# Attention in delta-rule form: triangles used as 32x32 tiles on TensorE's diagonal instead of block-diagonal 128x128 copies

## The chip, the cores and the metric

One NeuronCore of a Trainium2 chip. The metric is the device time of one execution in microseconds (us): 1447.51 us as the median of 3 runs (1442.47 to 1449.78) for the kernel before. TensorE (PE) multiplies and accumulates into PSUM, VectorE (DVE), ScalarE (ACT) and GpSimd (POOL) work elementwise, SyncE (SP) issues most DMAs. Every engine takes its own instructions in order.

## What is computed

The reference is a delta-rule attention, then two mixtures of experts (an argmax-gated one of 8 experts, a dense one of 4):

```python
for t in range(S):                      # S = 768, 32 heads (4 x 8), D = 48
    kt, vt, bt = k_n[:, :, t], v[:, :, t], beta[:, :, t, None]
    y[:, :, t] = einsum('bhd,bhde->bhe', q[:, :, t], state)
    v_old = einsum('bhde,bhd->bhe', state, kt)
    state = state + bt[..., None] * einsum('bhd,bhe->bhde', kt, vt - v_old)
x = moe(x)    # one expert of 8 per token: relu(x @ w1[e]) @ w2[e], times two gates
x = moe2(x)   # four experts, weighted by domain_probs
```

## The kernel before

The recurrence is done by blocks of 32 tokens. `run` walks 6 chunks of 128 tokens (c), each of 4 steps of 32 tokens (st = 4c+s), in two head groups (g). For a block of 32 tokens the state's updates are a triangular system, so the kernel inverts a 32x32 triangle for each head and block: `gram` makes the triangles' entries on PE, `inverse` (L339) runs the elimination on DVE, 31 columns one after another (L356, L357), two buffers deep (`NX`), between a first transpose (L344) and a last one (L380). Beside the inverse X each head has a second triangle P (from q and k). Both are split into two fp16 halves, high by ACT and low by POOL (by DVE for the first chunk), and written to the dense tile `TPd` ([128, 2, 4, 16, 32]: f is a pair of steps, the index of 4 is X high, X low, P high, P low). A partition holds 4 heads' rows, 32 each.

`stage_t` (L395) copies `TPd` to one of two block-diagonal tiles `TP`, for each pair of steps by 4 DMAs from SP, one for each quarter of the partitions, so that a 128x128 weight holds four heads' triangles and zeros elsewhere. `zero` clears the two tiles once.

A step's chain (`chain`, L411): `inject` puts v into PSUM (L409), L424 subtracts keys times state (weights `KT`), ACT and DVE split the result into r16, L432 multiplies by the inverse (weights `TP`), ACT and DVE split that into u16, L444 updates the state (weights `kb`), ACT and DVE make S16 for the next step. `outputs` (L448) makes y: L461 with `QT` and S16, L467 with P (`TP`) and u16. Each product has three matmuls (`HL`): high by high, low by high, high by low. L432 is given in two parts: 8 matmuls on r16's high half, 4 on its low half.

The order on all engines is not the source's: each piece of work is registered by `op` with a duration in ns, a priority and what it reads and writes, and `Plan.order` simulates the engines and emits instructions in that order. A step's chain is urgent, the inversion has a priority of 25 steps ahead, `OFF` shifts single pieces. A copy by `stage_t` counts `TPX` = 900 ns in that plan, a matmul `PEN` = 25 or `PY` = 43. Where PE would stand idle, the plan puts in matmuls on zeros (L195).

The attention takes the first 470 us of the span, then follow the two mixtures with plans of their own. Their buffers lie where the attention's were.

Of the kernel before, what the change touches and what calls it, by code (L numbers as in the profile page):

```python
# [7 lines left out]
F16 = mybir.dt.float16  # L8
# [3 lines left out]
ALU = mybir.AluOpType  # L12
# [3 lines left out]
B, H, S, D = 4, 8, 768, 48  # L16
# [25 lines left out]
TPX = 900  # L42
# [8 lines left out]
NX = 2  # L51
# [106 lines left out]
class Attention:  # L158
# [7 lines left out]
    def __init__(self,ctx,tc,plan,q,k,v,beta,kq,wa,wb,done,nsc=NSC):  # L166
# [4 lines left out]
        T=lambda n,s,d=F32: c.tile(s,d,name=n)  # L171
# [166 lines left out]
    def inverse(self,c):  # L338

        TPv=self.TPd.rearrange("p f w (s u) i -> p f w s u i",s=2)  # L340
        nc=self.nc; G,Pm,TPd,X,GZ=self.GT,self.Pm,self.TPd,self.X[c%NX],self.GX[c%NX]; xi=c%NX; t=f"inv {c}"; self.prio=4*c-LEAD[3]
        Pf=Pm.rearrange("p (u f s) i -> p f s u i",f=2,s=2)
# [63 lines left out]
    def inject(self,st,g):
# [44 lines left out]
    def outputs(self,st,g):  # L451
        nc=self.nc; s=st%4
        qt=self.QT[st%self.RQ]; tpt=self.TP[st//2%self.RT]; tp=lambda w,u: tpt[:,w,8*(s%2)+u]
        us=range(4*g,4*g+4); o=4*g; t=f"out {st} {g}"; self.prio=st+0.3
        S16=self.S16[g][st%2]; ko=('S16',g,st%2); u16=self.u16[g][st%2]; ku=('u16',g,st%2); cy=('cp',g,0)
        yp=self.cp[g][0][:,0,0:8*D].rearrange("p (u a d) -> p u a d",a=2,d=D)
        for half in range(2):
            uh=us[2*half:2*half+2]
            def qs(uh=uh):
                for u in uh:  # L460
                    for a,b in self.HL: nc.tensor.matmul(out=yp[:,u-o],lhsT=qt[:,a,u],rhs=S16[:,b,u-o],start=(u,a,b)==(o,0,0),stop=False,skip_group_check=True)  # L461
            if st>0: self.op('P',6*PY,qs,self.QTk(st)+[ko+(x,p) for x in range(2) for p in range(2)],[cy],t)
        for half in range(2):
            uh=us[2*half:2*half+2]
            def pu(uh=uh):
                for u in uh:
                    for a,b in self.HL: nc.tensor.matmul(out=yp[:,u-o],lhsT=tp(2+a,u),rhs=u16[:,b,u-o:u-o+1].to_broadcast([128,2,D]),start=(st,u,a,b)==(0,o,0,0),stop=b==1,skip_group_check=True)  # L467
            self.op('P',6*PY,pu,self.TPk(st)+[ku+(0,),ku+(1,)],[cy],t)
        ys=self.ys[st%2]
        for pp in range(2):  # L470
            R=slice(64*pp,64*pp+64)
            self.act(211,ys[R,o:o+4],yp[R,:,pp],[cy],[('ys',st%2,g,pp)],t,scale=-1.0/512)

    def run(self):
        n=self.nsc; L=4*n
        self.load_b(0); self.loads(0); self.setup(); self.keys(0); self.gram(0); self.inverse(0)
        for i in range(3): self.load_v(i)
        self.stage_k(0); self.stage_t(0); self.stage_q(0); self.stage_q(1)
        if n>1: self.load_b(1); self.loads(1); self.keys(1); self.gram(1)
        for c in range(n):  # L480
            for s in range(4):
                st=4*c+s
                if s==0: self.stage_t(st+2)
# [11 lines left out]
                if s==2 and c+1<n: self.stage_t(st+2); self.stage_q(st+2)  # L495
def bc(ap,shape,axis):
# [531 lines left out]
```

## Time and profile before

| | |
|---|---|
| median of 3 runs | 1447.51 us |
| profiled execution: time, span | 1452.08 us, 1450.5 us |
| PE busy, matmuls | 1289.6 us (89%), 14904 |
| DVE, ACT, POOL busy | 930.2, 690.9, 714.4 us |
| mean granted TensorE clock | 0.927 of full |

The span runs from the first to the last instruction. The chain of waits goes back from the last instruction to whatever released it, and so on. Busy shares are means over stages with different limits; what counts in a stage is who ends last there.

### The profile page before, as it was taken

What the parts mean: (1) busy time and instruction counts of PE and PEld (TensorE: products, weight loads), DVE (VectorE), ACT (ScalarE), POOL (GpSimd) and SP (SyncE); (2) the same over time, 40 slices, a digit from 0 to 9 for tenths busy, and PEclk for the clock granted to TensorE, in tenths of its full rate; (3) what the DMA queues carried; (4) which work ended last, traced back from release to release, by engine and by line L of the source; (5) the groups of instructions that cost most, each with busy time, mean ns of one, the idle gap of its engine ahead of it and who ended that gap; (6) DMA issues with size and microseconds to landing.
All of it is one profiled execution on the core that took longest, in us unless ns stands there. A gap on an engine that the chain in (4) does not pass through costs nothing.

```text
span 1450.5 us, 35997 instructions
## 1 busy us (share of the span) xinstructions
PE 1289.6 (89%) x14904; PEld 1066.8 (74%) x14904; DVE 930.2 (64%) x1877; ACT 690.9 (48%) x1348; POOL 714.4 (49%) x927
## 2 busy tenths in 40 slices
PE   7677686777778798899989999999999999999997
PEld 4355475665566654455679999899998999999997
DVE  7979888859745556653285556855578555564654
ACT  2846464645464444542254444544445444444433
POOL 3445554533223478310185445744468444456664
PEclk8688878868889999999999999999999999999999
DMA  8968988794797786763220102101121011011200
GB/s 124 184 94 159 109 132 113 124 128 84 123 116 128 190 226 173 211 177 101 74 63 23 45 23 87 46 23 35 33 77 34 23 34 34 23 36 54 66 34 34
DMA packets 358888, 130.48 MB, mean 90 GB/s; under 512 B 314688, under 2 KB 348992, under 8 KB 358720
## 3 DMA queue, kind: packets, MB, share of 16 engines
q1 hardware_dynamic: 351856, 112.69, 40.4%
q0 software_dynamic: 6864, 15.45, 3.3%
q8 instruction: 118, 1.93, 0.6%
q14 instruction: 50, 0.41, 0.1%
HBM read 76.38 MB, written 14.96 MB: 63 GB/s over the span
## 4 chain that ended last, share of the span: by engine, by line
PE 50%; DVE 13%; DMA 11%; issue 11%; SPq 5%; POOL 5%; ACT 4%; another core or an unknown queue 0%; POOLq 0%; ACTq 0%; DVEq 0%
PE b L928 23%; PE b L947 20%; SPq L215 4%; DMA s<-in_moe_w_dram 4%; DMA TP<-TPd 4%; DVE tmp L356 2%; DMA kq<-wa 2%; PE b L800 1%; POOL q L775 1%; DVE KT L306 1%; POOL S L936 1%; DVE X L357 1%; DVE wa L357 1%; PE Sp L444 1%; DVE v L753 1%
## 5 line engine op out<-in xcount | busy, mean ns | idle before, releaser
L928 PE MATMUL b<-wb,v 128*128 128x256 f16 x3456 | 392.8, 273 | 0.3 <-ACT a L930 0.2
L928 PEld LDWEIGHTS <-v 128*128 128x128 f16 x3456 | 336.7, 98 | 37.9 <-issue 0.9
L947 PE MATMUL b<-v,h 128*128 128x192 f16 x4032 | 353.5, 247 | 11.6 <-DVE cc L955 6.4
L947 PEld LDWEIGHTS <-h 128*128 128x128 f16 x4032 | 338.7, 98 | 16.6 <-issue 8.6
L936 POOL TENSOR_TENSOR S<-a 128x256 f32<-128x256 f32 x192 | 149.7, 800 | 272.7 <-ACT a L930 272.5
L940 DVE TENSOR_TENSOR h<-a,h 128x768 f16<-128x768 f32 x96 | 135.0, 1407 | 145.8 <-ACT h L939 138.3
L940 DVE TENSOR_TENSOR h<-S,h 128x1024 f16<-128x1024 f32 x96 | 120.9, 1259 | 125.6 <-ACT h L939 125.6
L939 ACT ACTIVATE h<-S 128x1024 f16<-128x1024 f32 x96 | 101.4, 1056 | 199.5 <-POOL S L936 179.8
L930 ACT ACTIVATE a<-b 128x512 f32<-128x512 f32 x192 | 113.4, 594 | 143.8 <-PE b L928 134.8
L936 POOL TENSOR_TENSOR S<-S,a 128x256 f32<-128x256 f32 x96 | 133.8, 1394 | 0.0
L195 PE MATMUL wp<-wz 128*128 128x512 f16 x304 | 85.4, 424 | 10.1 <-DVE LG L556 7.4
L939 ACT ACTIVATE h<-a 128x768 f16<-128x768 f32 x96 | 80.8, 842 | 2.8
L936 POOL TENSOR_TENSOR S<-a,S 128x256 f32<-128x256 f32 x96 | 73.7, 768 | 7.2
L195 PEld LDWEIGHTS <-wz 128*128 128x128 f16 x398 | 40.6, 107 | 47.0 <-issue 18.0
L203 ACT ACTIVATE QT<-kq 64x512 f16<-64x512 f16 x96 | 60.0, 626 | 11.4 <-PE cp L461 6.5
L815 POOL DMA_DIRECT2D x<-y x27 | 19.7, 733 | 90.5 <-DVE y L813 80.8
L432 PE MATMUL cp<-r,TP 128*128 128x48 f16 x576 | 31.4, 198 | 36.8 <-DMA TP<-TPd 20.6
L803 DVE SCALAR_TENSOR_TENSOR h<-b,h 128x432 f16<-128x432 f32 (+2 forms) x72 | 39.6, 552 | 36.2 <-ACT h L802 35.3
L444 PE MATMUL Sp<-u,kb 64*128 64x48 f16 x1152 | 35.4, 193 | 29.4 <-DVE S L449 15.2
L955 DVE TENSOR_TENSOR cc<-b,sm 128x192 f32<-128x192 f32 x192 | 58.5, 345 | 3.1 <-ACT sm L952 3.1
L753 DVE SCALAR_TENSOR_TENSOR v<-s,v 128x512 f16<-128x512 f32 (+2 forms) x56 | 45.5, 840 | 23.0 <-ACT v L752 21.1
L550 POOL TENSOR_TENSOR ys<-ys,sc 128x384 f32<-128x384 f32 x24 | 20.9, 871 | 79.7 <-ACT xr L203 36.0
(249 smaller groups left out, 2145.6 us busy)
## 6 DMA issues: line engine op xcount, KB each, us to landing
wb<-x SPq DMA_DIRECT2D x72, 256.0 KB
s<-in_moe_w_dram SPq DMA_DIRECT2D x40, 384.0 KB
s<-in_moe_w_dram SPq DMA_DIRECT2D x18, 512.0 KB
TP<-TPd SPq DMA_DIRECT2D x48, 128.0 KB
s<-in_moe_w_dram SPq DMA_DIRECT2D x24, 256.0 KB
v<-in_v_dram SPq DMA_DIRECT2D x96, 48.0 KB
xd<-xr SPq DMA_DIRECT2D x24, 192.0 KB
x<-y POOLq DMA_DIRECT2D x21, 216.0 KB
```

The costliest lines, as they stand in the source:

```text
L195: nc.tensor.matmul(out=out,lhsT=wz[:,0:128],rhs=wz[:,0:out.shape[1]],start=start,stop=True,skip_group_check=True)
L203: self.op('A',dur,lambda: self.nc.scalar.activation(out=out,in_=in_,func=func,scale=scale),reads,writes,tag,**k)
L215: self.op(q,occ,(lambda: e.dma_start_transpose(out=out,in_=in_)) if turn else (lambda: e.dma_start(out=out,in_=in_)),reads,list(writes)+[( ...
L444: for a,b in ps: nc.tensor.matmul(out=Sp[:,pp,u],lhsT=kb[R,a,u],rhs=u16[R,b,u-o],start=(st,u,a,b)==(0,0,0,0),stop=last and b==1,skip_group ...
L753: self.op('V',69+1.042*n,lambda: self.nc.vector.scalar_tensor_tensor(out=lo,in0=s,scalar=64.0,in1=hi,op0=ALU.mult,op1=ALU.subtract),reads+ ...
L928: for c,y in PASS: nc.tensor.matmul(out=F[k][:,f],lhsT=w[:,c,d,c_:c_+128],rhs=self.xk[B%2][d][:,y,256*i:256*i+256],start=(f,z)==(0,0),stop ...
L930: self.op('A',620,lambda k=k,g=g: A.activation(out=a[ja][:,g].rearrange("p x t -> p (x t)"),in_=F[k].rearrange("p a t -> p (a t)"),func=AF ...
L936: self.op('G',750,lambda o=o,x=x,y=y,w=w: G.tensor_tensor(out=X[o],in0=X[x],in1=X[y],op=w),ka,[ks])
L939: self.op('A',200+.833*m,lambda h=h,q=q,g=g: A.activation(out=h[:,0,:,q],in_=g,func=AF.Copy),kg,[kh+(0,)])
L940: self.op('V',200+1.042*m,lambda h=h,q=q,g=g: V.tensor_tensor(out=h[:,1,:,q],in0=g,in1=h[:,0,:,q],op=ALU.subtract),kg+[kh+(0,)],[kh+(1,)])
L947: for z,(c,d) in enumerate(PASS): nc.tensor.matmul(out=Q[k][:,o,0:192],lhsT=h[:,c,g,x],rhs=w[:,d,m,y],start=(m,o,z)==(0,0,0),stop=(m,z)==( ...
L955: self.op('V',340,lambda o=o,k=k,y=y,x=x: V.tensor_tensor(out=o,in0=Q[k][:,y,0:192],in1=s[:,x],op=ALU.add),[('Q',k),('sm',z,x)],[ko])
```

## The change

`TP`, `stage_t` and the copies are gone. PE takes the triangles from `TPd` directly, with 4 matmuls for each one of before, each with a weight of 32 rows and 32 columns at partitions 32q and an output at the same partitions. `TPd` is now two tiles, one for even and one for odd chunks. The plan counts 12 ns for one such matmul. `OFF` is the same.

```diff
-        self.TP=[T(f"TP{i}",[128,4,16,128],F16) for i in range(self.RT)]
-        self.TPd=T("TPd",[128,2,4,16,32],F16)
+        self.TPd=[T(f"TPd{i}",[128,2,4,16,32],F16) for i in range(2)]
...
+    def diagonal(self,out,w,st,rhs,us,ps,start,n=1):
+        tp=self.TPd[st//4%2][:,st%4//2]; x=8*(st%2); o=us[0]-us[0]%4
+        for u in us:
+            for a,b in ps:
+                for q in range(4):
+                    R=slice(32*q,32*q+32); r=rhs[R,b,u-o]; r=r if n==1 else rhs[R,b,u-o:u-o+1].to_broadcast([32,n,D])
+                    self.nc.tensor.matmul(out=out[R,u-o],lhsT=tp[R,w+a,x+u],rhs=r,start=start and (u,a,b)==(o,0,0),stop=b==1,skip_group_check=True)
+    def TDk(self,st,w): return [('TPd',st//4%2,st%4//2,x) for x in (w,w+1)]
...
-    def stage_t(self,st):
-        c,s=divmod(st,4); self.prio=st-2; sl=st//2%self.RT; tp=self.TP[sl]; f=s//2
-        self.zero(tp,('TP',sl),[('TP',sl,q) for q in range(4)],'G' if sl else 'V')
-        for qq in range(4):
-            R=slice(32*qq,32*qq+32)
-            self.dma(tp[R,:,:,32*qq:32*qq+32].rearrange("p w u i -> p (w u) i"),self.TPd[R,f].rearrange("p w u i -> p (w u) i"),[('TPd',f,w) for w in range(4)],[('TP',sl,qq)],f"tp {st}",xfer=TPX)
...
-                    for a,b in ps: nc.tensor.matmul(out=up[:,u-o],lhsT=tp(a,u),rhs=r16[:,b,u-o],start=(u,a,b)==(o,0,0),stop=b==1,skip_group_check=True)
-            self.op('P',4*len(ps)*PEN,mm,self.TPk(st)+[kr+(x,)],[cu],t,**U)
+            self.op('P',16*len(ps)*12,lambda ps=ps,x=x: self.diagonal(up,0,st,r16,list(us),ps,x==0),self.TDk(st,0)+[kr+(x,)],[cu],t,**U)
...
-                    for a,b in self.HL: nc.tensor.matmul(out=yp[:,u-o],lhsT=tp(2+a,u),rhs=u16[:,b,u-o:u-o+1].to_broadcast([128,2,D]),start=(st,u,a,b)==(0,o,0,0),stop=b==1,skip_group_check=True)
-            self.op('P',6*PY,pu,self.TPk(st)+[ku+(0,),ku+(1,)],[cy],t)
+            self.op('P',24*12,lambda uh=uh: self.diagonal(yp,2,st,u16,list(uh),self.HL,st==0,2),self.TDk(st,2)+[ku+(0,),ku+(1,)],[cy],t)
```

In the program PE has 4608 pairs of weight load and matmul at the new line L397 for the 1152 pairs of L432 and L467, and 321 matmuls on zeros for 398. SP has 48 DMAs fewer.

In a step of the second chunk a weight load and a matmul of L432 (`TP_98`, 128x48) stood 8 times in a row on PE, then, behind matmuls of the other group, 4 times; now a pair of L397 (`TPd_112`, 32x48) stands there 32 and then 16 times.

ACT at the start of the second chunk (`TPd<-Pm` is P's high half of the next chunk, `u` the high half of u16, `S` that of the state), before and then now:

```order
L203 ACTIVATE wa<-qf 128x8x48 x4
L203 ACTIVATE TPd<-Pm 128x512
L203 ACTIVATE u_122<-cp_141 128x192
L203 ACTIVATE u_124<-cp_143 128x192
L203 ACTIVATE S_127<-Sp 128x4x48 x2
```

```order
L202 ACTIVATE TPd_112<-GX_108 128x512 x2
L202 ACTIVATE TPd_111<-Pm 128x512
L345 ACTIVATE X_109<-b_88 128x32
L202 ACTIVATE GT<-gp_138 128x8x32
L202 ACTIVATE Pm<-gp_138 128x8x32
L202 ACTIVATE QT_96<-kq 64x16x32
L202 ACTIVATE u_121<-cp_140 128x192
```

The write of the next chunk's P goes to the other tile now and has moved ahead, right behind the writes of this chunk's X.

SP at the start of the second chunk, before and then now:

```order
L215 DMA_TRANSPOSE kq<-wa 128x32x128
L215 DMA TP_98<-TPd 32x64x32 x4
L215 DMA v_116<-in_v_dram 32x8x48 x4
L215 DMA xd<-xr_152 128x768
L215 DMA xd<-xr_150 128x768
L215 DMA xd<-xr_151 128x768
L215 DMA TP_99<-TPd 32x64x32 x4
L215 DMA_TRANSPOSE kb_114<-KT_93 128x16x128
```

```order
L214 DMA_TRANSPOSE kq<-wa 128x32x128
L214 DMA_TRANSPOSE kb_113<-KT_93 128x16x128
L214 DMA v_116<-in_v_dram 32x8x48 x4
L214 DMA_TRANSPOSE kb_114<-KT_94 128x16x128
L214 DMA v_117<-in_v_dram 32x8x48 x4
L214 DMA_TRANSPOSE kq<-wa 128x32x128
```

The transposes of keys (`kb`, `kq`) stand closer together and no longer behind copies.

## Rows read from the trace of the kernel before

**Rows 1.** The page's chain that ended last, shares of the span by line.

```profile
PE b L928 23%; PE b L947 20%; SPq L215 4%; DMA s<-in_moe_w_dram 4%; DMA TP<-TPd 4%; DVE tmp L356 2%; DMA kq<-wa 2%; PE b L800 1%; POOL q L775 1%; DVE KT L306 1%; POOL S L936 1%; DVE X L357 1%; DVE wa L357 1%; PE Sp L444 1%; DVE v L753 1%
```

**Rows 2.** Windows, attention and ten us of it: us, busy us by engine, clock, DMA.

```profile
core 0: us, PE busy (x) PEld busy (x) DVE busy (x) ACT busy (x) POOL busy (x), PEclk, DMA share, GB/s
83.00:470.00 387.00, 289.93 (x5352) 232.16 (x5351) 292.56 (x771) 212.71 (x547) 163.76 (x208) 0.81 0.83 122
...
252.00:262.00 10.00, 8.74 (x246) 7.66 (x244) 9.74 (x24) 9.33 (x26) 5.15 (x6) 1.00 0.96 147
```

**Rows 3.** Chain of waits in order of time, 80 to 470: start us, us, what.

```profile
92.79 6.05 DMA TP<-TPd
...
153.43 5.27 DMA TP<-TPd
...
164.31 13.09 DMA TP<-TPd
...
298.05 14.26 DMA kq<-wa
...
365.61 10.11 DMA TP<-TPd
...
420.10 11.83 DMA kb<-KT
```

**Rows 4.** Who waited for whom, 50 to 470: us, times, longest us.

```profile
ACT TPd L203 <- DMA TP<-TPd: 42.7, 8, 13.4
...
PE cp L432 <- DMA TP<-TPd: 20.6, 5, 8.8
...
PEld L424 <- issue: 13.3, 47, 0.6
```

**Rows 5.** Timeline of DVE: start us, us, line, operation, [idle before <-releaser].

```profile
93.09 0.84 DVE L436 SCALAR_TENSOR_TENSOR u<-cp,u 128x192 f16<-128x192 f32 x2 [1.80 <-ACT u L203]
...
178.38 0.36 DVE L436 SCALAR_TENSOR_TENSOR u<-cp,u 128x192 f16<-128x192 f32 x1 [4.34 <-ACT u L203]
...
243.63 0.36 DVE L206 TENSOR_TENSOR r<-cp,r 128x192 f16<-128x192 f32 x1 [3.85 <-ACT r L203]
...
292.26 0.83 DVE L436 SCALAR_TENSOR_TENSOR u<-cp,u 128x192 f16<-128x192 f32 x2 [2.88 <-ACT u L203]
...
376.83 0.84 DVE L436 SCALAR_TENSOR_TENSOR u<-cp,u 128x192 f16<-128x192 f32 x2 [5.85 <-ACT u L203]
```

**Rows 6.** Timelines of DVE, POOL and PE at the last chunk's start.

```profile
402.29 1.98 DVE L380 STREAM_TRANSPOSE GX<-X 128x1024 f32<-128x1024 f32 x1
...
405.94 2.27 POOL L206 TENSOR_TENSOR TPd<-GX,TPd 128x512 f16<-128x512 f32 x2 [8.46 <-ACT TPd L203]
...
418.26 1.12 PE L432 MATMUL cp<-r,TP 128*128 128x48 f16 x24 [2.38 <-DMA TP<-TPd]
```

**Rows 7.** DMA, 92 to 465: packets, and one group of issues.

```profile
DMA packets 220981, 46.18 MB, mean 124 GB/s; under 512 B 215095, under 2 KB 220060, under 8 KB 220924
...
TP<-TPd SPq DMA_DIRECT2D x42, 128.0 KB
```

**Rows 8.** Timeline of PE, 250 to 275.

```profile
254.26 0.36 PE L432 MATMUL cp<-r,TP 128*128 128x48 f16 x8
...
254.96 0.44 PE L424 MATMUL cp<-S,KT 128*64 128x48 f16 x16
255.33 0.27 PE L432 MATMUL cp<-r,TP 128*128 128x48 f16 x4
255.53 0.31 PE L424 MATMUL cp<-S,KT 128*64 128x48 f16 x8
...
258.49 0.67 PE L467 MATMUL cp<-u,TP 128*128 128x96 f16 x12
...
262.91 0.42 PE L467 MATMUL cp<-u,TP 128*128 128x96 f16 x6
```

**Rows 9.** Windows, the matmuls on zeros (L195) alone: us, PE, PEld, clock.

```profile
83.00:470.00 387.00, 54.15 (x213) 21.49 (x212) 0.81 0.83 122
```

More of the change, by code (lines that the diff above doesn't have):

```diff
@@ L338, in inverse @@
     def inverse(self,c):
-        TPv=self.TPd.rearrange("p f w (s u) i -> p f w s u i",s=2)
-        nc=self.nc; G,Pm,TPd,X,GZ=self.GT,self.Pm,self.TPd,self.X[c%NX],self.GX[c%NX]; xi=c%NX; t=f"inv {c}"; self.prio=4*c-LEAD[3]
+        TPv=self.TPd[c%2].rearrange("p f w (s u) i -> p f w s u i",s=2); it=c%2
+        nc=self.nc; G,Pm,TPd,X,GZ=self.GT,self.Pm,None,self.X[c%NX],self.GX[c%NX]; xi=c%NX; t=f"inv {c}"; self.prio=4*c-LEAD[3]
         Pf=Pm.rearrange("p (u f s) i -> p f s u i",f=2,s=2)
@@ L383, in inverse @@
             pk=[('Pm',2*f),('Pm',2*f+1)]
-            self.act(520,TPv[:,f,2],Pf[:,f],pk,[('TPd',f,2)],t)
-            self.tt(EL,DL,TPv[:,f,3],Pf[:,f],TPv[:,f,2],ALU.subtract,pk+[('TPd',f,2)],[('TPd',f,3)],t)
+            self.act(520,TPv[:,f,2],Pf[:,f],pk,[('TPd',it,f,2)],t)
+            self.tt(EL,DL,TPv[:,f,3],Pf[:,f],TPv[:,f,2],ALU.subtract,pk+[('TPd',it,f,2)],[('TPd',it,f,3)],t)
         Xf=XT.rearrange("p (u f s) i -> p f s u i",f=2,s=2)
         for f in range(2):
-            self.act(520,TPv[:,f,0],Xf[:,f],[kg],[('TPd',f,0)],t)
-            self.tt(EL,DL,TPv[:,f,1],Xf[:,f],TPv[:,f,0],ALU.subtract,[kg,('TPd',f,0)],[('TPd',f,1)],t)
+            self.act(520,TPv[:,f,0],Xf[:,f],[kg],[('TPd',it,f,0)],t)
+            self.tt(EL,DL,TPv[:,f,1],Xf[:,f],TPv[:,f,0],ALU.subtract,[kg,('TPd',it,f,0)],[('TPd',it,f,1)],t)
+    def diagonal(self,out,w,st,rhs,us,ps,start,n=1):
[6 more added lines that the diff above has]
+    def TDk(self,st,w): return [('TPd',st//4%2,st%4//2,x) for x in (w,w+1)]
     def stage_k(self,st):
@@ L403, in stage_q @@
         self.spread(st,1,self.QT[st%self.RQ],'QT',SPQ,f"Qsp {st}")
-    def TPk(self,st): return [('TP',st//2%self.RT,q) for q in range(4)]
     def inject(self,st,g):
@@ L412, in chain @@
         nc=self.nc; s=st%4; last=st==4*self.nsc-1
-        kt=self.KT[st%self.RK]; tpt=self.TP[st//2%self.RT]; tp=lambda w,u: tpt[:,w,8*(s%2)+u]; kb=self.kb[st%2]
+        kt=self.KT[st%self.RK]; kb=self.kb[st%2]
         us=range(4*g,4*g+4); o=4*g; t=f"ch {st} {g}"; self.prio=st; U=dict(urgent=True)
@@ L429, in chain @@
         for x,ps in enumerate((self.HL[:2],self.HL[2:])):
-            def mm(ps=ps):
-                for u in us:
-                    for a,b in ps: nc.tensor.matmul(out=up[:,u-o],lhsT=tp(a,u),rhs=r16[:,b,u-o],start=(u,a,b)==(o,0,0),stop=b==1,skip_group_check=True)
-            self.op('P',4*len(ps)*PEN,mm,self.TPk(st)+[kr+(x,)],[cu],t,**U)
+            self.op('P',16*len(ps)*12,lambda ps=ps,x=x: self.diagonal(up,0,st,r16,list(us),ps,x==0),self.TDk(st,0)+[kr+(x,)],[cu],t,**U)
         u16=self.u16[g][st%2]; ku=('u16',g,st%2)
@@ L452, in outputs @@
         nc=self.nc; s=st%4
-        qt=self.QT[st%self.RQ]; tpt=self.TP[st//2%self.RT]; tp=lambda w,u: tpt[:,w,8*(s%2)+u]
+        qt=self.QT[st%self.RQ]
         us=range(4*g,4*g+4); o=4*g; t=f"out {st} {g}"; self.prio=st+0.3
@@ L464, in outputs @@
             uh=us[2*half:2*half+2]
-            def pu(uh=uh):
-                for u in uh:
-                    for a,b in self.HL: nc.tensor.matmul(out=yp[:,u-o],lhsT=tp(2+a,u),rhs=u16[:,b,u-o:u-o+1].to_broadcast([128,2,D]),start=(st,u,a,b)==(0,o,0,0),stop=b==1,skip_group_check=True)
-            self.op('P',6*PY,pu,self.TPk(st)+[ku+(0,),ku+(1,)],[cy],t)
+            self.op('P',24*12,lambda uh=uh: self.diagonal(yp,2,st,u16,list(uh),self.HL,st==0,2),self.TDk(st,2)+[ku+(0,),ku+(1,)],[cy],t)
         ys=self.ys[st%2]
@@ L477, in run @@
         for i in range(3): self.load_v(i)
-        self.stage_k(0); self.stage_t(0); self.stage_q(0); self.stage_q(1)
+        self.stage_k(0); self.stage_q(0); self.stage_q(1)
         if n>1: self.load_b(1); self.loads(1); self.keys(1); self.gram(1)
@@ L482, in run @@
                 st=4*c+s
-                if s==0: self.stage_t(st+2)
                 if s==0 and c+1<n: self.inverse(c+1)
@@ L494, in run @@
                 self.done(st,self.ys[st%2].rearrange('p u d -> p (u d)'),[('ys',st%2,g,pp) for g in range(2) for pp in range(2)])
-                if s==2 and c+1<n: self.stage_t(st+2); self.stage_q(st+2)
+                if s==2 and c+1<n: self.stage_q(st+2)
 def bc(ap,shape,axis):
```

## The prediction

> **What bounds the kernel now.** I read the chain of waits by line first. Its two large entries are the matmuls of the second mixture (L928, L947), which the change doesn't touch; of what it touches, the copy TP<-TPd stands there with 4% [rows 1]. Then the windows of the attention: between 83 and 470 us PE is busy 290 of 387 us, DVE 293, the DMA engines 0.83 of the time [rows 2]. No engine is full, so the waits matter. The chain in order of time has six waits for the copy, first at 92.79 (6.05 us) and last at 365.61 (10.11 us), about 51 us in all [rows 3]. They lie at the chunks' starts: the inversion of chunk c ends on DVE, ACT and POOL write TPd, SP issues four DMAs among its other work, and only then may L432 begin.
>
> The copy also holds up ACT. TPd is one tile, so P's high half of the next chunk can't be written before the copy has read this one. ACT stood 42.7 us before these writes, 8 times, against 20.6 us in which PE itself stood before L432 [rows 4]. Behind the write in ACT's queue stand the high halves of u, r and the state, and behind those in DVE's queue the steps of the inversion, which depend on nothing of this.
>
> What would bound the stretch without the copy is the inversion. It is one long chain on DVE for each chunk, and chunk c+1 can't start before it. So the 51 us aren't all to be had: most of them lie beside an inversion that goes on meanwhile. What counts is the time in which the copy stopped DVE too, and the time behind the last inversion.
>
> **Removed: the copy.** DVE stood idle behind the copy five times while an inversion was under way: 1.80, 4.34, 3.85, 2.88 and 5.85 us, each before a u or r whose ACT half came late [rows 5]. Together 18.7 us. In each case L432, or the write to TPd ahead of it on ACT, had just been released by the copy. The last inversion ends with the transpose at 402.29. POOL writes the low halves from 405.94, two in 2.27 us, so the first pair of steps has its X at about 407.1. L432 starts at 418.26 [rows 6]. In between lies only the copy, if the fourth chunk's steps, which themselves come earlier, are done: 11.2 us. Sum of the gain: 29.9 us. Bounds: nothing (each wait turns into another one), and 51 us (all of the copy's share of the chain).
>
> What is late next at a chunk's start is POOL's subtraction for the low half, which now feeds L397 directly. It is contained in the 407.1 above.
>
> Also gone are 48 DMA issues on SP and their transfers, 12% of the bytes between 92 and 465 us (42 x 128 KB of 46.18 MB). Pieces of 64 bytes make that 42 x 2048 = 86016 of 220981 packets, 39% [rows 7]. Behind them waited the transposes of keys, which have 14.26 and 11.83 us in the chain [rows 3]. I count nothing for it, from below nothing and from above half of these two, 13 us. The zeroing of TP, at the start while the first keys are being loaded, I also count at nothing.
>
> **Added: a second TPd tile.** The write of P for the next chunk waits for the readers of the chunk before this one, which are a whole chunk old. Behind it on ACT stand u, r and S as before; cost nothing.
>
> **Added: 3456 more pairs on PE.** No row shows a 32x32 weight. The nearest are these [rows 8], at a granted clock of 1.00 [rows 2]. A 128x128 weight with 48 columns: 8 in 0.36 us and 4 in 0.27, so 22.5 ns each. With 96 columns (L467): 12 in 0.67 and 6 in 0.42, 42 ns each. A weight of half the array's columns (L424), where two neighbours use different halves: 16 in 0.44 and 8 in 0.31, 16 ns each. So two tiles side by side overlap, and a pair of instructions can go out at least every 16 ns. Four tiles on the diagonal could overlap fourfold, 22.5/4 or 42/4, some 6 to 10 ns: the lower bound. The upper is no overlap, 22.5 and 42 ns. I take 16 ns, as the nearest row has it.
>
> For one step and group: the part on r16's high half grows from 8 x 22.5 = 180 to 32 x 16 = 512 ns, but its low half comes only 1.07 us after the first part began (254.26 to 255.33), so this is covered. The second part grows from 4 x 22.5 = 90 to 16 x 16 = 256, by 166 ns. The outputs grow from 12 x 42 = 504 to 48 x 16 = 768, by 264 ns. Together 430 ns, 48 times, 20.6 us of PE. PE has 97 us idle there [rows 2] and 54 us of matmuls on zeros [rows 9], and nothing in a step's chain waits for the outputs; I let a third reach the end: 6.9 us.
>
> Changing the weight's shape costs something: weight loads of L424 stood 13.3 us in 47 waits with no releaser, 0.28 us each, behind matmuls of the full array [rows 4]. One more such change in each step and group is 48 x 0.28 = 13.4 us. Mostly PE stands waiting for r16 there anyway; I take a quarter, 3.4 us. If the cover is gone it is all of it.
>
> The Trainium skill (TensorE: Matmul & The Clock Gate, "Wait — 56ns, not 53.3ns?") says that matmuls never start closer than about 25 ns apart, however few columns they have. By that the new matmuls would cost 48 x ((16 x 25 - 90) + (48 x 25 - 504)) = 48 us of PE, and the gain would be used up. The trace disagrees: L424 has 16 ns [rows 8]. I stay with the row.
>
> **Sum.** 29.9 - 6.9 - 3.4 = 19.6 us less. The profiled execution took 1452.1 us (span 1450.5), so 1432.5 on its scale. The runs' median is 4.6 us lower, 1447.5, which gives 1428. The clock, a mean of 0.81 in this stretch [rows 2] between its two levels, I take as unchanged, although there are fewer matmuls on zeros. The mixtures have plans of their own and only shift.
>
> **The rivals.**
> - More than that: the DMA engines are the hidden limit. For it: the share of 0.83, the copy's 39% of packets, and the transposes in the chain. Against it: most transposes land in time. Gain 19.6 plus 13 plus the rest of ACT's 42.7 us in part, some 12: about 45, 1403.
> - No change: the plan orders afresh with shifts that belonged to the old order, and the waits come back as others, for gram's result, for keys, or behind the last steps for the experts' weights. For it: a chain with many short links. Against it: the copy is in that chain six times. Time 1441 to 1454.
> - Slower: the quarter tiles don't overlap, and PE takes 22.5 and 42 ns for each as for a full weight. Then a step and group costs 12 x 22.5 + 36 x 42 = 1.78 us more, 85 us of PE in all, which fills its 97 idle us. Half of it and all changes of shape reach the end: 43 + 13 against 30, so 26 us slower, 1474. It decides from about 20 ns a matmul, where 24 x (64 x 20 - 594) ns and 13 us make up the gain. For it: no row with four tiles. Against it: the overlap of two in L424. By the floor of 25 ns of the Trainium skill's TensorE page it would be 1455.
>
> **How the numbers follow.** Forecast 0.52 (its own range 1408 to 1440), more 0.18, no change 0.14, slower 0.16. This kernel's runs tell 0.5% from no change, that is 7 us, 1440 to 1455. So faster 0.70, same 0.14, slower 0.16. The range goes from 1400, which leaves out a third of the second case, to 1455, which leaves out most of the slow one.
>
> **What would show it.** In the profile after: no wait for a copy; ACT's write of P without a wait before it; DVE's idle time before u and r shorter at the chunks' starts; the last chunk's first L397 about 1 us behind POOL's first subtraction; attention's end some 20 us earlier. A block of 16 matmuls at L397 should take about 0.18 + 15 x 0.016 = 0.42 us, and 48 pairs under 1 us. The prediction is wrong if these blocks take twice that, if the clock in the stretch falls clearly below 0.81, or if DVE's idle time stays at 94 of 387 us.

## The result: no gain, 0.55% slower, and attention ends 12 us later

The changed kernel took 1453.7 us (median of 10 runs, 1446.95 to 1463.5), the kernel before 1445.3 on the same chip (10 runs, 1442.47 to 1449.78): ratio 1.0055, 95% interval 1.0033 to 1.0078. 1428 was forecast, 1400 to 1455 as the range, and 0.16 stood on "slower". The execution profiled took 1458.21 us, its span is 1456.6.

Attention's end is read from the matmul that counts the tokens. Its row before and after (minimum, median and maximum ns, then first and last start us):

```profile
L620 PE MATMUL wp<-run,ones x1: 166/166/166, 471.6 to 471.6; 128*128 128x8 f16 x1
```

```profile
L614 PE MATMUL wp<-run,ones x1: 167/167/167, 483.9 to 483.9; 128*128 128x8 f16 x1
```

So 12.3 us are lost in the attention, and the mixtures give back 6.2 of them (span less this start: 978.9 us before, 972.7 after). The windows of the changed kernel, columns as in [rows 2]; the second line is the matmuls on zeros (L194) alone, which answers to [rows 9]:

```profile
83.00:470.00 387.00, 302.51 (x8367) 237.94 (x8367) 284.93 (x749) 208.62 (x528) 154.80 (x197) 0.76 0.63 106
```

```profile
83.00:470.00 387.00, 42.45 (x149) 16.08 (x149) 0.76 0.63 106
```

The copies are gone and the DMA engines are relieved (0.63 for 0.83). PE is busy 12.6 us longer though 11.7 us of zeros are missing, the clock is 0.76 for 0.81, and DVE's idle time is 102 us where it was 94: two of the three signs by which the prediction was to be judged wrong.

The waits after, 75 to 484 us (who waited for whom: us, times, longest us), answer to [rows 4]:

```profile
PEld L397 <- issue: 41.5, 47, 2.6
DVE S L447 <- ACT S L202: 30.4, 21, 7.2
PE cp L397 <- issue: 26.4, 27, 3.0
ACT u L202 <- PE cp L397: 25.2, 23, 2.8
...
DVE u L434 <- ACT u L202: 23.9, 18, 5.4
PEld L425 <- issue: 23.1, 51, 4.7
...
PE cp L425 <- issue: 8.8, 7, 4.9
...
ACT TPd L202 <- DVE GX L379: 6.9, 1, 6.9
```

For comparison, two lines of the kernel before (75 to 472 us):

```profile
PEld L432 <- issue: 35.6, 28, 9.3
...
DVE S L449 <- ACT S L203: 14.1, 14, 2.1
```

No wait for a copy is left, and ACT's writes of TPd wait for the inverse itself. In their place stands "PE <- issue": TensorE stops before L397 and L425 with no semaphore to wait for. The weight loads' line has a like one before (35.6 us); the 26.4 us of the matmuls at L397 have none. ACT waits for these matmuls, and DVE for ACT, above all for the state S (30.4 us where it was 14.1), so the inversion on DVE goes on later each time. The last chunk shows it (timelines of DVE, POOL and PE):

```profile
419.78 1.94 DVE L379 STREAM_TRANSPOSE GX<-X 128x1024 f32<-128x1024 f32 x1
...
423.60 2.28 POOL L205 TENSOR_TENSOR TPd<-GX,TPd 128x512 f16<-128x512 f32 x2
...
424.52 1.23 PE L397 MATMUL cp<-r,TPd 32*32 32x48 f16 x96
```

Against [rows 6], L397 follows POOL's start by 0.92 us where L432 followed by 12.32. That step came as forecast. But the inversion ends 17.49 us later, so the chunk starts 6.3 us later than before. The first chunk had started 14 us earlier (first L397 at 78.2, first L432 at 92.05).

How TensorE stops is seen in its timeline at the first chunk (start us, us, line, operation, count, [idle before <-releaser]):

```profile
85.47 0.53 PE L397 MATMUL cp<-r,TPd 32*32 32x48 f16 x48
...
87.65 0.27 PE L397 MATMUL cp<-r,TPd 32*32 32x48 f16 x13
88.93 0.42 PE L397 MATMUL cp<-r,TPd 32*32 32x48 f16 x35 [1.01 <-issue]
89.17 0.70 PE L397 MATMUL cp<-u,TPd 32*32 32x96 f16 x48
...
91.05 0.30 PE L397 MATMUL cp<-u,TPd 32*32 32x96 f16 x9
93.75 0.60 PE L397 MATMUL cp<-u,TPd 32*32 32x96 f16 x39 [2.41 <-issue]
```

A block of 48 pairs that isn't stopped takes 0.53 us with 48 columns, 0.70 with 96; full tiles took 0.36 + 0.27 and 0.67 for the same work [rows 8]. The tiles themselves overlap well. But a block can be cut in the middle, behind 13 or 9 pairs, for 1 to 2.4 us. The page's line of the queue that loads code names the suspect, first before, then after:

```profile
q8 instruction: 118, 1.93, 0.6%
```

```profile
q8 instruction: 144, 2.36, 0.7%
```

These are blocks of 16 KB. TensorE has 29896 and 36658 instructions in the two traces, 116.8 and 143.2 times 256, so nearly all of this queue is its code. I numbered TensorE's instructions in the trace (weight loads, matmuls, its few others) and took each number modulo 256. In the changed kernel 14 of the 33 stalls over 0.35 us lie at the same remainder, 194, and so do all that the timeline above shows. By this a block of code holds 256 instructions, 128 pairs; the long runs below test it.

The theory from this: **supply.** TensorE runs out of instructions, since the change puts 6912 more of them into the attention. Its rivals: **order** (the plan, made anew with shifts that belonged to the old order, is worse), **shape** (quarter tiles cost by themselves), **clock** (0.76 for 0.81), and that the copies had been hidden anyway.

### The profile page after: what moved, and what is told of

Read it like the earlier page. It is cut to its first block, busy times and chain, and to the rows that moved or that the text cites. A ratio compares the mean times of both kernels' runs of the same rounds, so it can differ in the third digit from the quotient of the medians.

```text
span 1456.6 us, 42688 instructions
## 1 busy us (share of the span) xinstructions
PE 1304.7 (90%) x18283; PEld 1079.3 (74%) x18283; DVE 921.5 (63%) x1873; ACT 692.4 (48%) x1348; POOL 711.9 (49%) x923
## 4 chain that ended last, share of the span: by engine, by line
PE 46%; issue 8%; DMA 5%; DVE 2%; POOL 2%; SPq 1%; ACT 1%; POOLq 0%; ACTq 0%; DVEq 0%
PE b L922 24%; PE b L941 22%; DMA s<-in_moe_w_dram 4%; SPq L740 1%; POOL S L930 1%; PE b L794 1%; POOL q L769 1%; DMA xt<-xg 1%; DVE v L747 1%; DMA xg<-xd,wid 0%; DVE h L934 0%; SPq L855 0%; DVE kq L747 0%; POOL xg L782 0%; POOL x L809 0%
## 5 line engine op out<-in xcount | busy, mean ns | idle before, releaser
L922 PEld LDWEIGHTS <-v 128*128 128x128 f16 x3456 | 336.6, 98 | 37.9 <-issue 0.8
L397 PEld LDWEIGHTS <-TPd 32*32 32x32 f16 x4608 | 60.2, 103 | 49.1 <-issue 41.5
L194 PE MATMUL wp<-wz 128*128 128x512 f16 x248 | 71.8, 437 | 4.8 <-DVE LG L550 2.9
L194 PEld LDWEIGHTS <-wz 128*128 128x128 f16 x321 | 33.6, 111 | 43.6 <-issue 18.9
L397 PE MATMUL cp<-u,TPd 32*32 32x96 f16 x2304 | 46.9, 233 | 16.9 <-issue 16.9
L809 POOL DMA_DIRECT2D x<-y x27 | 19.7, 728 | 86.0 <-DVE y L807 76.1
L797 DVE SCALAR_TENSOR_TENSOR h<-b,h 128x432 f16<-128x432 f32 (+2 forms) x72 | 39.5, 553 | 33.6 <-ACT h L796 33.1
L747 DVE SCALAR_TENSOR_TENSOR v<-s,v 128x512 f16<-128x512 f32 (+2 forms) x56 | 45.5, 837 | 21.9 <-ACT v L746 18.5
```

The source lines that it names most:

```text
L194: nc.tensor.matmul(out=out,lhsT=wz[:,0:128],rhs=wz[:,0:out.shape[1]],start=start,stop=True,skip_group_check=True)
L397: self.nc.tensor.matmul(out=out[R,u-o],lhsT=tp[R,w+a,x+u],rhs=r,start=start and (u,a,b)==(o,0,0),stop=b==1,skip_group_check=True)
L747: self.op('V',69+1.042*n,lambda: self.nc.vector.scalar_tensor_tensor(out=lo,in0=s,scalar=64.0,in1=hi,op0=ALU.mult,op1=ALU.subtract),reads+ ...
L797: self.op('V',69+1.042*n,lambda ps=ps,h=h: nc.vector.scalar_tensor_tensor(out=h[:,1],in0=ps,scalar=0.0,in1=h[:,0],op0=ALU.max,op1=ALU.subt ...
L922: for c,y in PASS: nc.tensor.matmul(out=F[k][:,f],lhsT=w[:,c,d,c_:c_+128],rhs=self.xk[B%2][d][:,y,256*i:256*i+256],start=(f,z)==(0,0),stop ...
```

## The experiments

All stalls below are counted in one way: TensorE idle over 0.35 us, no semaphore on the instruction behind or ahead, from 75 us to attention's end. "Edge" is the remainder 194, which is the same in every kernel, since the code starts alike. Each end is that of one profiled execution, and ten executions of the changed kernel lie between 1446.95 and 1463.5 us, so a few us between two ends are not told apart.

```
kernel                              end us  instr.  us per 256  stalls us (n)  at the edge
before: copies, full tiles          471.6   10961   9.26         5.9  (8)       1.8  (2)
changed: new order, quarter tiles   483.9   17765   5.89        35.2 (33)      19.2 (14)
old order, no copies, quarter       481.6   17922   5.81        41.4 (23)      35.5 (20)
old order, copies, quarter          496.5   17810   6.06        40.3 (29)      31.7 (25)
old order, no copies, full          433.7   11010   8.34         0.8  (1)       0.8  (1)
new order, no copies, full          431.3   10816   8.43         1.6  (2)       1.1  (1)
quarter, fewer pairs                459.3   12167   8.09         5.3  (8)       1.2  (1)
quarter, fewer pairs, more zeros    453.6   12573   7.71         9.2  (7)       4.6  (4)
full, fewer pairs                   437.9    9521   9.76         3.4  (4)       1.4  (1)
full, half the zeros                439.6   10783   8.66         6.7  (4)       4.3  (2)
X quarter, P copied                 454.6   14459   6.72        29.9 (29)       8.0  (7)
P quarter, X copied                 473.8   14509   7.04        19.7 (21)       5.3  (4)
X quarter in the first pair only    447.1   12796   7.44        19.8  (8)      14.5  (7)
```

### The order and the tiles taken apart

**Quarter tiles in the old order.** The plan still holds the copies' times and dependencies, so the order of ACT, DVE and POOL is that of before; only nothing is copied.

```diff
-        self.TP=[T(f"TP{i}",[128,4,16,128],F16) for i in range(self.RT)]
-        self.TPd=T("TPd",[128,2,4,16,32],F16)
+        self.TPd=[T(f"TPd{i}",[128,2,4,16,32],F16) for i in range(2)]
...
-            self.dma(tp[R,:,:,32*qq:32*qq+32]...,xfer=TPX)
+        ... no=lambda: None
...
+            r=[('TPd',f,w) for w in range(4)]; i=len(self.pl.ops)
+            self.op('D',500,no,r,[('TP',sl,qq),('tok',i)],t,lat=450)
+            self.op('X',TPX,no,r+[('tok',i)],[('TP',sl,qq)],t,lat=XS)
...
+            self.op('P',4*len(ps)*PEN,lambda ps=ps,x=x: self.diagonal(up,0,st,r16,list(us),ps,x==0),self.TPk(st)+[kr+(x,)],[cu],t,**U)
```

> The plan of the kernel before (same durations, dependencies and priorities, so the same order on DVE, ACT and POOL), but no copies: quarter tiles read from two TPd tiles. Supply theory (TensorE starves on four times the instructions): stalls of PE with nothing to wait for stay at 25 to 40 us of the attention, attention's end (the counts matmul) at 478 to 490 us, time 1448 to 1458, like the changed kernel. Order theory (the loss comes from the new order of the plan, not from the tiles): attention's end at 455 to 466 us, time 1425 to 1440. If the copies were hidden and the tiles cost nothing: 1442 to 1449.

Measured: ratio 1.0131 (1.0083 to 1.0179), attention's end 481.6 us, within 2.3 us of the changed kernel; the stalls (41.4 us) and the median (1460.09 us) lie 1.4 and 2.1 us above what supply expected. In this trace ACT takes the instructions of the kernel before in the same order, and DVE and POOL too, but for the zeroing of TP. Order is out as the cause of the loss: by the ratios the new order is even the better one (1.0055 and 1.0131). The stalls by line (PE alone, columns as above):

```profile
PE cp L397 <- issue: 26.1, 18, 4.4
...
PE cp L468 <- issue: 7.1, 4, 5.1
PE Sp L451 <- issue: 6.6, 5, 1.9
...
PE gp L326 <- issue: 4.8, 2, 4.5
```

L468 (query by state), L451 (the state's update) and L326 (gram) are matmuls that the change didn't touch: a block of code ends wherever it ends, and whatever stands there waits. At the edge lie 20 of the 23 stalls, 35.5 of 41.4 us.

**No copies, full tiles, old order.**

```diff
-                    for a,b in ps: nc.tensor.matmul(out=up[:,u-o],lhsT=tp(a,u),rhs=r16[:,b,u-o],...)
+        ... tp=lambda w: self.TPs[:,w] ...
+                ms=[nc.tensor.matmul(out=up[:,u-o],lhsT=tp(a),rhs=r16[:,b,u-o],...) for u in us for a,b in ps]
+                if x==0: self.after(ms[0],st,(0,1))
```

> The old order without the copies and with the old full 128x128 matmuls: their weights are constant diagonals (so the real triangles are left out of the products and the routing of the mixtures differs), but they still wait for ACT's and POOL's writes of TPd. Supply theory: stalls of PE with nothing to wait for at most 10 us, attention's end at 448 to 460 us against 471.6 before, the gain that the prediction counted. Copies-hidden theory: attention's end within 4 us of 471.6. Read by attention's end, since the mixtures get other tokens.

Measured: attention's end 433.7 us, 37.9 ahead of the kernel before and 14 ahead of what supply expected, ratio 0.9744 (0.9698 to 0.9789), stalls 0.8 us. The copies were not hidden; without them the attention gains more than the 29.9 us of the prediction. This is the one line of PE's stalls that is left:

```profile
PE cp L476 <- issue: 0.8, 1, 0.8
```

**Copies kept, quarter tiles.** The four diagonal blocks of TP are read as quarter tiles.

```diff
+        tp=self.TP[st//2%self.RT]; x=8*(st%2)
...
+                    self.nc.tensor.matmul(out=out[R,u-o],lhsT=tp[R,w+a,x+u,R],rhs=r,...)
```

> The kernel before with its copies and its order, but the matmuls read the four 32x32 diagonal blocks of TP as quarter tiles. Supply theory: only the cost is left, stalls of PE with nothing to wait for 25 to 40 us in the attention, attention's end at 480 to 495 us, time 1453 to 1468. Order theory: quarter tiles cost little, attention's end within 4 us of 471.6, time 1442 to 1450.

Measured: ratio 1.0221 (1.0182 to 1.0260), attention's end 496.5 us, 24.9 behind the kernel before, stalls 40.3 us; median (1470.69 us), end and stalls lie a little above what supply expected. The waits for the copy are still there, and the stalls beside them:

```profile
PE cp L398 <- issue: 17.8, 16, 3.1
PE cp L398 <- DMA TP<-TPd: 17.5, 6, 7.2
PE cp L432 <- issue: 8.2, 5, 4.5
...
PE Sp L449 <- issue: 5.9, 7, 1.8
```

**The new order with full tiles.** The changed kernel's plan, with `diagonal` emitting one full pair with constant weights for four quarter pairs.

> The changed kernel's plan and order, no copies, but full 128x128 matmuls with constant diagonals for weights (real triangles left out, routing differs), which wait for ACT's and POOL's writes. Supply theory: stalls of PE with nothing to wait for at most 10 us, attention's end at 455 to 474 us, 10 us or more before the 484.3 of the changed kernel. Order theory: attention's end stays at 479 to 487 us. Read by attention's end.

Measured: attention's end 431.3 us, ratio 0.9724 (0.9678 to 0.9770), 24 us ahead of what supply expected. With full tiles the two orders end 2.4 us apart. So a square of four, in the old order: taking the copies away is worth 37.9 us with full tiles and 14.9 with quarter tiles (496.5 to 481.6); quarter tiles cost 24.9 us beside the copies and 47.9 without them. Stalls differ by 40.6 us where the end differs by 47.9, 34.7 of them at the edge. In the new order the end differs by 52.6 us (483.9 and 431.3) and the stalls by 33.6, 18.1 of them at the edge.

Stalls do not simply add to the end. From 75 us to the end, without copies and in the old order, quarter tiles keep TensorE busy 35.5 us longer (320.3 and 284.8, weight loads included), and it waits 30.5 us less for semaphores (42.6 and 73.1). The 4085 matmuls beside triangles and zeros, the same in both kernels, take 196.9 and 174.8 us of that, at a granted clock of 0.81 and 0.86. So part of the 47.9 us is the clock; how much is not separated.

### The supply by itself

**Two long runs of pairs** at the start of the kernel before, on zeros, with nothing to wait for.

```diff
+        for k in range(1024):
+            q=k%4; R=slice(32*q,32*q+32); nc.tensor.matmul(out=wp[R,0,0:48],lhsT=wz[R,0:32],rhs=wz[R,0:48],...)
+        for k in range(1024): nc.tensor.matmul(out=wp[:,0,0:48],lhsT=wz[:,0:128],rhs=wz[:,0:48],...)
```

> The kernel before with two runs of pairs on zeros put at its start: 1024 quarter-tile pairs (32x32 weights, 48 columns, the four tiles of the diagonal in turn), then 1024 full 128x128 pairs of 48 columns, neither waiting for anything. Supply theory: the quarter pairs do not go on at the 7 ns of a short block; after the first blocks of 256 instructions they stop at each block's edge for about 2 us and need 3.4 to 5 us a block (27 to 40 ns a pair), and full pairs, at 22 ns or more, need 3 to 5 us a block as well, with shorter stops. Rival (the stalls belong to the tile shape or to the waits of the attention): the 1024 quarter pairs pass in 7 to 12 us without stops at the edges.

Measured, PE's timeline of one profiled run:

```profile
1.37 2.42 PE L197 MATMUL wp<-wz 32*32 32x48 f16 x223 [1.37 <-DVE s L232]
6.49 1.47 PE L197 MATMUL wp<-wz 32*32 32x48 f16 x128 [2.69 <-issue]
11.04 1.47 PE L197 MATMUL wp<-wz 32*32 32x48 f16 x128 [3.08 <-issue]
15.31 1.47 PE L197 MATMUL wp<-wz 32*32 32x48 f16 x128 [2.81 <-issue]
19.59 1.60 PE L197 MATMUL wp<-wz 32*32 32x48 f16 x128 [2.81 <-issue]
23.59 1.47 PE L197 MATMUL wp<-wz 32*32 32x48 f16 x128 [2.40 <-issue]
27.05 1.47 PE L197 MATMUL wp<-wz 32*32 32x48 f16 x128 [1.99 <-issue]
31.60 0.51 PE L197 MATMUL wp<-wz 32*32 32x48 f16 x33 [3.09 <-issue]
...
40.15 3.36 PE L198 MATMUL wp<-wz 128*128 128x48 f16 x128 [1.19 <-issue]
43.88 3.36 PE L198 MATMUL wp<-wz 128*128 128x48 f16 x128 [0.37 <-issue]
```

Behind the first 223 pairs come bursts of exactly 128 pairs, 1.5 to 1.6 us long, and 2.0 to 3.1 us of nothing in between; an edge every 3.45 to 4.55 us, 27 to 36 ns a pair, though a pair takes 10 ns inside the burst. Full pairs of 48 columns take 3.36 us a block and still wait 1.19 us at one edge and 0.37 at three of eight; at the other four it is 0.1 us or less.

The clock of the quarter run has to be read from the full pairs behind it. The trace has no record of the granted clock before 34.5 us, where 1.00 begins (in the other traces the records begin at 4.0 to 7.2 us), and the windows print 1.00 for a stretch without records. Two windows of 2 us on the full pairs, before and behind 34.5 us:

```profile
32.20:34.20 2.00, 2.00 (x54) 2.00 (x53) 0.00 (x0) 0.00 (x0) 0.00 (x0) 1.00 0.99 208
36.00:38.00 2.00, 2.00 (x87) 2.00 (x83) 0.00 (x0) 0.00 (x0) 0.00 (x0) 1.00 1.11 172
```

From start to start a full pair takes 40 ns up to 34.5 us and 25 ns from there. So the quarter run most likely went at the lower of the two levels (1.2 GHz), and the full pairs behind 34.5 us at the upper (2.4 GHz). The stops don't need the lower level: of the 14 stalls at the edge in the changed kernel, 11 end at a granted clock of 1.00.

The code loads of the trace lie in between in a fixed way:

```
edge 6.49   load 8.62 + 0.93     edge 11.04  (1.49 behind the load's end)
edge 11.04  load 12.98 + 0.92    edge 15.31  (1.41)
edge 15.31  load 17.24 + 0.96    edge 19.59  (1.39)
edge 19.59  load 20.98 + 1.19    edge 23.59  (1.42)
```

The load that ends the stop starts 1.2 to 2.2 us after TensorE has entered the block ahead of it (all six full bursts), takes about 1 us, and TensorE goes on 1.4 to 1.5 us behind its end. In the attention it is the same: at all 14 stalls at the edge in the changed kernel TensorE goes on 1.2 to 1.7 us behind a load's end, and at all 20 of the quarter tiles in the old order 1.2 to 1.6; at the changed kernel's four stalls over 1 us away from the edge it is 2.4 to 5.5. The Trainium skill (Runtime: NRT & Kernel Launch, Instruction fetch mechanics) describes blocks of 16 KiB with 256 instructions, fetched through a queue of the engine's own while the block before runs, and calls the cost of an edge mostly hidden. Size and queue agree with the trace; hidden holds here only while 256 instructions last longer than the 3.45 to 4.55 us from edge to edge.

**Fewer quarter pairs.** Nearly only high by high, 36 of 96 pairs.

```diff
-            for a,b in ps:
+            for a,b in [(0,0)]*((0,0) in ps)+[(0,1)]*(n==1 and u==o and (0,1) in ps):
```

> As the quarter tiles in the old order, but of the three products of high and low halves nearly only high by high is done (36 of 96 quarter pairs a stage and group of heads; the low products are left out, one of them kept so that the wait for DVE's low half stays). TensorE then has 1152 instructions more than the full tiles without copies, instead of 6912. Supply theory (number of instructions): stalls at block edges at most 8 us, attention's end at 432 to 445 us. Tile-shape theory (the four-tile blocks themselves cost, as at each change of shape): a third or more of the 48 us is left, attention's end at 448 to 465 us.

Measured: ratio 0.9939 (0.9922 to 0.9956); the stalls fall to 5.3 us, as supply has it, but attention's end is 459.3 us, outside what supply expected and inside what the shape theory did. Supply is not all of it.

### What stalls don't explain

**Full tiles with the same fewer products.**

```diff
-for u in us for a,b in ps]
+for u in us for a,b in [(0,0)]*((0,0) in ps)+[(0,1)]*(u==o and (0,1) in ps)]
```

> The no-copy kernel with full tiles and constant diagonals, with the same products left out as in the quarter-tile kernel with fewer pairs (9 full pairs instead of 24 a stage and group of heads). That quarter-tile kernel ended its attention at 459.3 us with only 5.3 us of stalls, at a granted clock of 0.70 (75 to 430 us), against 433.7 us and 0.86 with all 24 full pairs. Clock theory (fewer columns streamed, lower clock, nothing to do with the tile's shape): clock 0.68 to 0.77 and attention's end at 448 to 462 us here too. Shape theory (quarter tiles cost 20 us by themselves, in drains or waits): clock 0.82 or more and attention's end at 425 to 438 us.

**Every second matmul on zeros left out of the kernel with full tiles.**

```diff
-                            ops.append(('P',dw,fn,(),0,False,0)); start.append(x); x+=dw/FR; break
+                            self.nf=getattr(self,'nf',0)+1
+                            if x<70000 or self.nf%2: ops.append(('P',dw,fn,(),0,False,0)); start.append(x)
+                            x+=dw/FR; break
```

> The no-copy kernel with full tiles and constant diagonals, with every second matmul on zeros left out from 70 us on (113 fewer), everything else the same. It prices the clock by itself: the granted clock of 75 to 430 us should fall from 0.86 to 0.68 to 0.78. Clock theory (the lower clock explains what stalls do not, 26 us between the quarter-tile kernel with fewer pairs at 0.70 and this one's parent at 0.86): attention's end at 446 to 462 us against 433.7. Rival (the clock matters little, quarter tiles cost by themselves): attention's end within 6 us of 433.7.

**More zeros beside the fewer quarter pairs**, by `FR = 1.6` for `FR = 0.95`.

> The quarter-tile kernel with fewer pairs (low products left out), with more matmuls on zeros set in the same gaps of the plan (650 instead of 398), everything else the same. Its parent ended its attention at 459.3 us at a granted clock of 0.70, PE busy or loading 316 of 384 us, with 5.3 us of stalls; the full-tile kernel with the same products had 437.9 us and 0.77. Clock theory (the remaining 20 us are the lower clock): clock 0.80 to 0.90, attention's end at 436 to 450 us although the zeros themselves take time. Shape theory (quarter tiles cost 20 us by themselves): attention's end at 455 to 465 us at whatever clock.

The windows 75 to 430 us, in the order fewer quarter pairs, the same with more zeros, fewer full pairs, half the zeros:

```profile
75.00:430.00 355.00, 290.07 (x5592) 217.70 (x5590) 282.44 (x727) 203.49 (x524) 157.62 (x202) 0.70 0.62 108
```

```profile
75.00:430.00 355.00, 306.84 (x5877) 224.25 (x5875) 291.79 (x742) 209.54 (x539) 160.37 (x206) 0.76 0.62 108
```

```profile
75.00:430.00 355.00, 277.03 (x4713) 213.85 (x4707) 298.74 (x764) 212.89 (x553) 162.86 (x211) 0.77 0.64 113
```

```profile
75.00:430.00 355.00, 269.69 (x5325) 219.36 (x5324) 298.79 (x762) 214.60 (x553) 163.63 (x211) 0.81 0.66 113
```

Attention's ends: 459.3, 453.6, 437.9 and 439.6 us; the ratios 0.9939 (above), 0.9958 (0.9928 to 0.9989), 0.9790 (0.9760 to 0.9821) and 0.9780 (0.9734 to 0.9826). None of the three came out clearly as either theory had it. The full tiles with fewer products fell to a clock of 0.77 as the clock theory said, and ended 4.2 us later only, with less to do. Half the zeros didn't bring the clock down far enough to price it (0.81); the end is 5.9 us later, just inside the rival's 6, and the stalls grew by as much. More zeros lifted the quarter tiles' clock to 0.76 and brought the end 5.7 us forward, but not the time (0.9958 and 0.9939). At like clock and with like products, quarter tiles end 15.7 us behind full ones (453.6 and 437.9), 5.8 of that in stalls. Whether the other 10 belong to the shape, to the added zeros, which take PE's time, or to the constant weights of the full-tile kernel is left open. With all products, 7.3 of the 47.9 us remain beside the stalls in the old order, and 19.0 of the 52.6 in the new.

### Quarter tiles for a part only

**X by quarter tiles, P copied**, and **P by quarter tiles, X copied**: the changed kernel with `TP` for two of the four words and the old matmul for them.

```diff
+        self.TP=[T(f"TP{i}",[128,2,16,128],F16) for i in range(self.RT)]
...
+            self.dma(tp[R,:,:,32*qq:32*qq+32].rearrange("p w u i -> p (w u) i"),self.TPd[it][R,f,2:4].rearrange("p w u i -> p (w u) i"),[('TPd',it,f,w) for w in (2,3)],[('TP',sl,qq)],f"tp {st}",xfer=500)
```

> The changed kernel with the inverse's triangles used as quarter tiles, but the triangles of the query products copied into block-diagonal form (half the copies) and used as full tiles. TensorE has 3456 instructions more than with full tiles throughout, half of the changed kernel's surplus. Supply theory: stalls at block edges 8 to 18 us, attention's end at 445 to 462 us, time 1415 to 1435, faster than both kernels. Rival (copies of the query part are late as before, or any quarter tile costs its share): attention's end at 460 to 475 us, time 1436 to 1450.

> The other half: the triangles of the query products as quarter tiles, those of the inverse copied into block-diagonal form. As many instructions as in the other half's kernel (3456 more than with full tiles), so the same stalls by the supply theory (8 to 18 us), but the copy of the inverse stands between POOL's last write and the first matmul of a pair of stages: attention's end 6 to 15 us behind the other half's kernel, at 455 to 472 us, time 1425 to 1445. Rival (the copies were no part of the path): attention's end within 4 us of the other half's kernel.

Measured: 0.9951 (0.9928 to 0.9975) with attention's end at 454.6 us, and 1.0017 (0.9993 to 1.0040) with 473.8. Times and ends are those of supply for the first, the second ends 1.8 us past its bound. With equally many instructions the two lie 19.2 us apart (6 to 15 expected). That fits a copy of X, which is ready last, on the path, and a copy of P, which is ready before the inversion, beside it; but each kernel has a plan of its own, and TensorE's own waits for the copy of X come to 4.3 us only. The stalls were under-forecast (29.9 and 19.7 us, 8 to 18 expected): at the edge lie 8.0 and 5.3, most are elsewhere; on those, the last section.

**X by quarter tiles only where its copy would be late**, in the first pair of steps of a chunk.

```diff
+            if s<2: self.op('P',16*len(ps)*12,lambda ps=ps,x=x: self.diagonal(up,0,st,r16,list(us),ps,x==0),self.TDk(st,0)+[kr+(x,)],[cu],t,**U)
+            else: self.op('P',4*len(ps)*PEN,mm,[('TX',q) for q in range(4)]+[kr+(x,)],[cu],t,**U)
```

> The kernel with the inverse's triangles as quarter tiles and the query triangles copied, changed so that the inverse's triangles are quarter tiles only in the first pair of stages of a chunk, where the copy would stand on the path; for the second pair they are copied too, two stages ahead. TensorE's surplus over full tiles falls from 3456 to 1728 instructions. Supply theory: stalls (edges and others) 5 to 16 us instead of 29.9, attention's end at 438 to 450 us against 454.6, time 1415 to 1430. Rival (the rest of that kernel's loss has another cause, the clock or the copies): attention's end at 450 to 460 us, time 1430 to 1438.

Measured: 1425.21 us (before 1438.49 on that chip), ratio 0.9907 (0.9879 to 0.9936), attention's end 447.1 us: faster than both kernels. Stalls 19.8 us, a little over what was expected, 14.5 of them at seven edges. One wait that ends with a copy is left (L459 itself reads `kb` and u, so what it is for stays open):

```profile
PE Sp L459 <- DMA TX<-TPd: 4.7, 1, 4.7
```

A second TPd tile in the kernel before, with the copies kept, wasn't tried. It would have told ACT's wait for the copy from TensorE's.

## Why the prediction was wrong

- **The step that failed is "Added: 3456 more pairs on PE".** It priced a pair by its pitch inside a block, let idle time and zeros cover two thirds, and had no term for fetching the code of 6912 more instructions. In place of its 6.9 us the runs showed stalls without a semaphore: 35.2 us in the changed kernel and 5.9 before, of which 19.2 and 1.8 lie at the edges of the code; in the square of four 40.6 more, 34.7 of them at the edges. The stalls away from the edges (16.0 us and 4.1 before) stay open. [Rows 4] were read for PE's waits without a releaser only as a change of shape, and the page's q8 line wasn't read at all: TensorE's 10961 instructions take a new block each 9.26 us in the attention, and four pairs for each one of the triangles make that 5.89, where a stretch without waits can have one in 3.45 to 4.55.
- The pitch itself was taken too high. 48 pairs take 0.53 us where 16 ns gave 0.93; the blocks of the triangles move the end of TensorE's work forward by 72.9 us in all against 62.0 before, 10.9 us and not 20.6. "PE has idle time" was no cover: the stalls fall into the blocks on the chain r, u, S.
- **Removed: the copy** was right in kind, and too small: 37.9 us with full tiles against 29.9, the waits of [rows 3] to [rows 5] gone, and the last chunk's start as worked out from [rows 6]. What the DMA engines' relief adds in it, which was counted at nothing, isn't separated.
- With quarter tiles the same step gains only 14.9 us; the two terms were added as if each had its own place on the path. From 75 us to the end, TensorE waits 17.1 us less for semaphores without the copies with full tiles (90.2 to 73.1) and 16.0 less with quarter tiles (58.6 to 42.6). What is missing lies in its busy time, 15.1 us shorter with full tiles (299.9 to 284.8) and 0.8 with quarter tiles (321.1 to 320.3), and in the stalls, 5.1 us less and 1.1 more. The granted clock rose from 0.815 to 0.857 with full tiles and from 0.802 to 0.811 with quarter tiles. That fits a clock that rises only where TensorE isn't stopped again, but no run separates it.
- The shape term (3.4) isn't shown by itself; the 7 to 19 us beside the stalls may hold it, and hold the clock too.
- The clock was taken as unchanged and fell to 0.76, with 42 us of zeros for 54 [rows 9]. That fall isn't the main cause: the quarter tiles in the old order have 0.80 and end as late. Against the full tiles without copies (0.86) the clock is a part of the loss.
- The rival "no change" had the time right by luck, since it put it down to a plan that orders badly. The order costs nothing (431.3 and 433.7; 483.9 and 481.6). The rival "slower" had tiles that don't overlap; they do. The floor of 25 ns that the Trainium skill states (TensorE: Matmul & The Clock Gate, "Wait — 56ns, not 53.3ns?") gave 1455, close to the result, by luck too: the full pairs of the long run stand at it (25 ns), but 48 quarter pairs in 0.53 us are under it, and the 27 to 36 ns of a long run come from its code.

## What to carry to other kernels

Price a change that splits matmuls in instructions, not only in array time: set TensorE's instructions in a stretch over 256 against its length, beside what the code loads of a run without waits allow (here one block in 3.45 to 4.55 us). "Issue" waits that cut a block of like matmuls in the middle, at equal distances of 256 instructions, are this limit in the runs here, and they fall on whatever line stands there. A cheaper form with more instructions belongs only where it saves a wait on the path: here the first pair of steps of a chunk, which kept a gain of 0.93%.

## What the runs showed of the hardware that was not expected

Quarter tiles on the diagonal overlap three- to fourfold. At a granted clock of 1.00, 48 pairs of 48 columns in the changed kernel stand 7 ns apart from start to start, against 25 for full pairs; at the lower level it is 10 ns against 40.

A second kind of stall shows mostly in kernels with quarter tiles, away from the edges: some four pairs, a stop of 0.4 to 0.5 us, and again. In the changed kernel (timeline, PE and POOL):

```profile
383.91 0.43 PE L397 MATMUL cp<-u,TPd 32*32 32x96 f16 x24
384.51 0.26 PE L397 MATMUL cp<-u,TPd 32*32 32x96 f16 x4 [0.16 <-issue]
...
385.08 0.97 POOL L575 DMA_INDIRECT ord<-rid,su  x1 [0.21 <-issue]
385.26 0.31 PE L397 MATMUL cp<-u,TPd 32*32 32x96 f16 x4 [0.49 <-issue]
...
386.01 0.29 PE L397 MATMUL cp<-u,TPd 32*32 32x96 f16 x4 [0.44 <-issue]
...
386.35 1.24 POOL L575 DMA_INDIRECT ord<-rid,su  x1 [0.23 <-issue]
...
386.77 0.28 PE L397 MATMUL cp<-u,TPd 32*32 32x96 f16 x3 [0.47 <-issue]
```

There are 16.0 us of stalls off the edge in the changed kernel, 21.9 with X alone as quarter tiles, 4.1 before. 15 of its 19 and 18 of those 22 lie within 0.3 us of one of POOL's 25 indirect DMAs, which with that margin cover about a tenth of the time; but they come in a few groups, and the quarter tiles in the old order have the same 25 indirect DMAs and no stop of 0.4 to 0.5 us. So whether the indirect DMAs slow TensorE, is open. So are single stops of 4.3 to 5.6 us away from any edge: two with X alone as quarter tiles, and one each in the changed kernel, with copies kept, with P alone and with X in the first pair.
